# The last chunk's product chain in one PSUM bank or in two, with the order of work rewritten

## The chip, the cores and the metric

The kernel runs on one core of a Trainium2 chip. The core has a matrix engine (TensorE, PE in the profile; PEld is its weight load), VectorE (DVE), ScalarE (ACT), GpSimd (POOL) and SyncE (SP), which only issues transfers. Each engine executes its own instructions strictly in the order given, and waits on semaphores for the others. TensorE writes its results to PSUM, eight banks of 512 fp32 values in each of 128 partitions; VectorE and ScalarE read them there. The other engines' data lie in SBUF. DMA queues move data between HBM and SBUF.

The metric is the device time of one execution in microseconds (us), the median of a few runs.

## The reference

Attention without a softmax over pairs, then a feed-forward block, on 8 batches, 8 heads, 576 tokens, 64 values per head:

```python
q_s = softmax(q, axis=-1)          # over the 64 values of a head
k_s = softmax(k, axis=2)           # over the 576 tokens
kv  = einsum('bhsd,bhse->bhde', k_s, v)
x   = einsum('bhsd,bhde->bhse', q_s, kv)   # to 4608 tokens x 512
h   = x @ w_in                     # 512 x 2048
out = (h * sigmoid(h)) @ w_out     # 2048 x 512, 4608 x 512 fp32
```

## The kernel before, in words

**Tiling.** The 4608 tokens are cut into nine chunks of 512, numbered 0 to 8. Batches have 576 tokens, so a chunk takes its tokens from one or two batches (`pieces`, L266). Chunk 0 is done in a wide form with the 576 tokens of batch 0. From chunk 1 on, the first matrix product, and for chunks 1 to 8 the second, are done by a seven-product scheme on halves (Strassen's in Winograd's form): two halves of the tokens, two of the inner dimension, two of the output, with seven products in place of eight and sums before and after.

**The order table.** The program has a list of named steps, `ORDER` (L18), and issues them one by one (L796). A step's engine is fixed by its function, or by a last letter of the name (`a` ScalarE, `v` VectorE; for stores `s` SyncE, `a` ScalarE, `g` GpSimd). So the table sets each engine's order; between engines only the data and the buffers do. The names that the prediction uses, with `t` a chunk, `b` a batch:

| step | engine | what it does | line |
|---|---|---|---|
| `lq`, `lk`, `lv` b.c | SP (POOL for b < 3) | load half of q, k, v of a batch; two buffers each | L150 |
| `eq`, `ek` b.c | ACT | exp of q, of k | L161, L166 |
| `z` b.c, `n` b.c | DVE, then POOL | sums of exp(q) and their reciprocals; the normalizing product on `eq` | L205, L209, L214 |
| `tq` b | SP | DMA transpose of `eq` to `qT` | L224 |
| `vc` b.c | POOL | cast of v to bf16 | L144 |
| `kv` b, `kc` b | PE, then DVE | k^T v of a batch; division by the sums of exp(k) | L246, L257 |
| `X` t.i | PE | x of the chunk, from `qT` and kv, to banks 0, 1, 6, 7 | L280 |
| `x` t.c, `xs` t.i | ACT or DVE; DVE | x to SBUF; the sums of its halves | L142, L144; L381 |
| `g` t.g.i | PE | product i of the first matrix product, group g; 8 matmuls | L423 |
| `s` t.g.i, `a` t.g.i, `u` t.g.i | ACT or DVE; DVE; ACT | snapshot of the running sum in banks 0 and 1; addition of another product; silu to `GT` | L142, L144; L401; L407 |
| `S` t.i | DVE | the sums of halves of `GT` | L475 |
| `b` t.i.m | PE | product i of the second matrix product for token quarter m of a half; 8 matmuls | L501 |
| `sa`, `sb`, `sc` t | ACT | snapshots of the running sum in bank 4 | L517 |
| `wa`, `wb`, `wc`, `wl` t, `o` t.m | DVE (`wl` either); SP | output sums; their stores | L521, L534, L536; L439 |
| `w`, `h`, `v`, `p`, `m`, `mu`, `tr1`, `T`, `WS`, `po`, `os` | | chunk 0's wide form, chunk 1's first part, batch 1's transposes on TensorE, sums of weights | L305 to L485 |

There is one buffer of `eq` (`exp_q`, L158), so `eq` b waits until batch b-1's transpose has landed. There are three output tiles `ow`; two of `qT`. `exp` and `silu` need different function tables of ScalarE, so each change from the one to the other puts an `ACT_TABLE_LOAD` in front; copies need none.

**PSUM.** The whole of PSUM is one tile, `PS`. Accesses of two engines to the same bank are put one after the other in the order of the program, even where they touch different columns.

**The last chunk.** Chunk 8 (`last`) has its own second product, steps `e` i.m, with i the product and m the half of a 256-token block (128 tokens). Products 1, 6, 7, 4 accumulate one after the other into bank 1 (halves in its two halves), and after 1, 6 and 7 the snapshots `sa8`, `sb8`, `sc8` are taken of the bank (L754). Product 5 goes to banks 4 and 0, 2 to bank 5, 3 to bank 6. Outputs are made in parts of 128 x 256: `waE` (1 + 2), `wxE` and `wbE` (1 + 6 + 5, then + 3), `wcE` (1 + 6 + 7 + 5) on VectorE (L760), and `wlE` (1 + 6 + 7 + 4), a scaled copy of bank 1 by ScalarE or VectorE (L773, L775). Each part is stored in two pieces of 64 rows by `qa`, `qb`, `qc`, `ql` (L778), on the queue that the name's last letter gives.

Of the kernel before, what the change touches and what calls it, by code (L numbers as in the profile page):

```python
# [15 lines left out]


ORDER = """  # L18
    lk1.0 w2 lk1.1 w0 h2 w1 h0 v2 w3 v0 h1 v1 W2b1 w4 h3 v3 w6 h4 WS0.1 w5 h6 WS1.1 W2b2 v4 w7 h5 v5 w8 h7
    v6 w9 lv1.0 h8 v7 WS0.2 w10 h9 v8 eq1.0.0 w11 v9 h10 eq1.0.1 w12 v10 h11 qp1a w13 eq1.1.0 v11 h12 WS0.4  # L20
    qp1b w14 h13 v12 lv1.1 w15 v13 W2c1 WS0.3 p0 W2c2 h15 z1.0 eq1.1.1 p1 v15 n1.0 h14 p2 v14 p3 z1.1.0
    gcopy lq2.0 z1.1.1 tr1.0 ek1.1 lq2.1 p4 n1.1 W2d ek1.0 p5 tc1.0b tc1.0a p6 T1 lk2.0 vc1.0 lk2.1 tr1.1
    WS1.3 p7 lv2.0 vc1.1a vc1.1b tc1.1a tc1.1b kv1 WS1.2 lv2.1 p8 kc1 xt1.0 xt1.1 x1.0a x1.1v p9 x1.2a x1.3v
    g1.1.1 xs1.3 eq2.0 xs1.1 xs1.2 g1.1.2 xs1.4 s1.1.0a z2.0 p10 eq2.1 g1.1.6 a1.1.0 n2.0 p11 s1.1.1a z2.1
    p12 g1.1.7 ek2.0 n2.1 g1.1.5 s1.1.2v p13 a1.1.2 ek2.1 g1.1.4 tq2 WS1.4 p14 vc2.0 p15 u1.1.4 g1.1.3 vc2.1
    po2v po0a lv3.0 m0 po1v u1.1.2 lk3.0 a1.1.1 m1 po3a lk3.1 mu0 lq3.0 m2 T2 mu1 lq3.1 u1.1.1 m3 os0 T4 m4
    mu2 u1.1.0 m5 T3 mu4 os1 kv2 mu5 mu3 m6 vc3.0 kc2 X2.0 mu6 X2.1 lv3.1 x2.1v m7 x2.0a x2.3a x2.2v g2.1.1
    mu7 xs2.1 xs2.2 b1.1.0 xs2.4 xs2.3 s2.1.0v g2.1.2 ek3.0 b1.2.0 S1.1 eq3.0 lk4.0 g2.1.6 lv4.0 S1.2 lq4.0
    b1.1.1 s2.1.1a a2.1.0 b1.2.1 eq3.1 g2.1.7 S1.3 sa1 vc3.1 g2.0.2 s2.1.2a g2.1.5 z3.1 ek3.1 lv4.1 b1.6.0
    lk4.1 a2.1.2 g2.1.4 n3.1 b1.6.1 z3.0 u2.1.4 g2.1.3 sb1 u2.1.0 g2.0.1 n3.0 a2.1.1 b1.7.0 s2.0.0a wa1 kv3  # L30
    u2.1.1 a2.0.0 tq3 g2.0.6 vc4.0 u2.1.2 b1.7.1 s2.0.1v vc4.1 b1.5.0 S1.4 g2.0.7 ek4.0 g2.0.5 sc1 s2.0.2v
    lk5.0 ek4.1 b1.5.1 kc3 eq4.0 g2.0.4 a2.0.2 b1.4.0 lq5.0 wc1 lq4.1 g2.0.3 z4.0 os3 u2.0.4 b1.4.1 lv5.0
    u2.0.0 a2.0.1 b1.3.0 n4.0 os2 wl1a X3.0 X3.1 lk5.1 kv4 x3.0a x3.1v x3.3a x3.2v b1.3.1 u2.0.2 kc4 g3.1.1
# [5 lines left out]
    n5.1 X4.0 X4.1 kv5 x4.0a x4.1v x4.3a wl2v b2.3.1 u3.0.0 x4.2v tq5 g4.1.1 xs4.3 u3.0.1 xs4.1 b3.1.0 wb2  # L39
    s4.1.0a xs4.2 g4.1.2 xs4.4 S3.1 b3.2.0 a4.1.0 ek6.0 g4.1.6 b3.1.1 S3.2 s4.1.1a lk7.0 o2.0 b3.2.1 sa3  # L40
    ek6.1 g4.1.7 g4.1.5 eq6.0 lv6.0 s4.1.2v b3.6.0 eq6.1 lq7.0 a4.1.2 lk7.1 b3.6.1 wa3 g4.1.4 lv6.1 kc5
    g4.1.3 S3.3 u4.1.4 g4.0.2 lq7.1 sb3 a4.1.1 u4.1.0 g4.0.1 z6.0 b3.5.0 s4.0.0a b3.7.0 u4.1.1 a4.0.0 n6.0
    g4.0.6 S3.4 b3.7.1 s4.0.1a g4.0.5 sc3 z6.1 u4.1.2 g4.0.7 vc6.1 b3.4.0 s4.0.2a n6.1 b3.5.1 u4.0.0 a4.0.2
# [10 lines left out]
    g6.0.4 a6.0.2 b5.4.1 u6.0.4 b5.3.0 X7.0 X7.1 x7.0a x7.1v g6.0.3 x7.3a x7.2v u6.0.2 g7.1.1 xs7.1 a6.0.1
    b5.3.1 s7.1.0a xs7.2 g7.1.2 u6.0.1 wl5v g7.1.6 o5.1 a7.1.0 g7.0.2 s7.1.1a xs7.4 xs7.3 b6.1.0 S6.1 o4.1
    b6.1.1 wb5 g7.1.7 sa6 b6.2.0 s7.1.2a g7.1.5 u7.1.0 g7.1.4 a7.1.2 o5.0 b6.2.1 u7.1.4 S6.2 g7.1.3 u7.1.2
    g7.0.1 a7.1.1 b6.6.0 s7.0.0a S6.3 b6.6.1 u7.1.1 wa6 g7.0.6 sb6 a7.0.0 b6.5.0 s7.0.1a b6.7.0 u7.0.0
    g7.0.7 b6.7.1 s7.0.2v g7.0.5 sc6 b6.5.1 a7.0.2 g7.0.4 S6.4 b6.4.0 u7.0.4 b6.4.1 u7.0.2 X8.0 wl6v X8.1
    x8.0a g7.0.3 wc6 x8.3a x8.2v b7.1.0 x8.1v b6.3.0 xs8.3 a7.0.1 b6.3.1 xs8.1 g8.1.1 u7.0.1 xs8.2 wb6
    g8.1.2 s8.1.0a xs8.4 o6.0 S7.1 b7.1.1 g8.1.6 a8.1.0 o6.1 b7.2.0 s8.1.1a S7.2 b7.2.1 sa7 S7.3 g8.1.7 S7.4  # L60
    g8.1.5 s8.1.2a b7.6.0 u8.1.0 a8.1.2 g8.1.4 b7.6.1 u8.1.4 g8.1.3 sb7 g8.0.1 a8.1.1 b7.7.0 s8.0.0a wa7
    b7.7.1 u8.1.1 b7.5.0 u8.1.2 g8.0.6 sc7 g8.0.2 s8.0.1a b7.5.1 a8.0.0 g8.0.7 u8.0.0 g8.0.5 s8.0.2v b7.4.0
# [8 lines left out]
def kernel(  # L71
# [683 lines left out]
    def tile_out(th, n, a):
        return w_out_tile(last, th)[:, a, n * HN:(n + 1) * HN]
# [9 lines left out]
            op1=ALU.add,  # L766
        )

    def part_copy(a, h, w, eng):
        o = tile_out(1, 0, a)[:, h * w:(h + 1) * w]  # L770
        i = PS[:, 1, a * HN + h * w:a * HN + (h + 1) * w]
        if eng is nc.scalar:
            nc.scalar.activation(out=o, in_=i, func=ACT.Copy, scale=OS)  # L773
# [54 lines left out]
```

## Time and profile before

| | |
|---|---|
| median of 3 runs | 259.99 us (259.85 to 260.35) |
| the profiled execution's own time | 259.86 us |
| its span, first to last instruction | 258.1 us |
| granted TensorE clock, mean | 0.995 |
| busy: PE, DVE, ACT, POOL | 249.7, 205.3, 188.5, 64.5 us |
| ACT_TABLE_LOAD | 14, of 1.28 us |

Busy time is the time in which an engine executes; its idle time is set down to what ended it, the releaser. A row of the order of time has the start, the duration, the engine, the line, the operation, output and inputs with their shapes, the count where several are merged, and in brackets the idle time before it with the releaser. An engine with a q, such as SPq, is its sequencer issuing a transfer. TensorE's matmuls overlap, so the end of a merged row can lie after the start of the next.

### The profile page before, as it was taken

To read this page: it belongs to the slowest core of one execution; us is meant where nothing else is said; L and a number is where in the kernel's file an instruction comes from. 1 tells how busy PE (TensorE), PEld (TensorE's weight loads), DVE (VectorE), ACT (ScalarE), POOL (GpSimd) and SP (SyncE) were. 2 spreads that over 40 slices of the span, in tenths; PEclk is the share of its full clock that TensorE was granted. 3 is DMA by queue.
4 is the path that set the end of the run, shared out by engine and by line. 5 is a ranking of instruction groups with operands and counts; after the bars stand their busy time and mean duration, and the time that the engine had idled before them with its cause. 6 is when DMAs were issued, how large, how long until landed. Compare 5 with 4: busy or idle time off the path is not lost.

```text
span 258.1 us, 6452 instructions
## 1 busy us (share of the span) xinstructions
PE 249.7 (97%) x2732; PEld 204.9 (79%) x2732; DVE 205.3 (80%) x278; ACT 188.5 (73%) x222; POOL 64.5 (25%) x62
## 2 busy tenths in 40 slices
...
GB/s 246 343 188 298 298 306 327 302 255 354 387 236 240 343 263 173 144 265 183 259 251 60 225 240 3 3 173 3 0 3 186 60 0 4 163 3 0 73 143 112
DMA packets 35996, 45.89 MB, mean 178 GB/s; under 512 B 16240, under 2 KB 21040, under 8 KB 35968
## 3 DMA queue, kind: packets, MB, share of 16 engines
...
q10 hardware_dynamic: 160, 0.13, 0.2%
...
## 4 chain that ended last, share of the span: by engine, by line
PE 83%; DVE 7%; DMA 4%; ACT 2%; issue 1%; SPq 1%; ACTq 0%; DVEq 0%
PE PS L501 33%; PE PS L423 31%; PE PS L305 6%; PE PS L443 5%; DMA vt<-in_v_dram 4%; PE PS L333 2%; PE PS L246 2%; PE PS L280 2%; DVE h L401 2%; DVE S L475 1%; DVE zq L205 1%; DVE h L144 1%; SPq L150 1%; DMA out_dram<-ow 1%; DVE ow L521 1%
## 5 line engine op out<-in xcount | busy, mean ns | idle before, releaser
L401 DVE TENSOR_TENSOR h<-PS,h 128x1024 f32<-128x1024 f32 (+1 forms) x45 | 54.1, 1205 | 16.8 <-PE PS L423 13.7
L501 PEld LDWEIGHTS <-GT 128*128 128x128 f16 x512 | 50.0, 98 | 5.8
L407 ACT ACTIVATE GT<-h 128x1024 f16<-128x1024 f32 (+1 forms) x45 | 46.7, 1050 | 8.9 <-DVE h L401 8.8
L423 PEld LDWEIGHTS <-WS 128*128 128x128 f16 x480 | 46.7, 98 | 6.7 <-issue 0.9
L501 PE MATMUL PS<-W,GT 128*128 128x256 f16 x384 | 48.0, 273 | 0.0
L423 PE MATMUL PS<-XS,WS 128*128 128x256 f16 (+1 forms) x360 | 44.5, 272 | 0.0
L142 ACT COPY h<-PS 128x1024 f32<-128x1024 f32 (+1 forms) x33 | 33.2, 1005 | 13.5 <-PE PS L423 11.8
L501 PEld LDWEIGHTS <-S 128*128 128x128 f16 x384 | 37.3, 98 | 4.4
L214 POOL TENSOR_TENSOR eq<-eq,rzq 128x1152 bf16<-128x1152 bf16 x13 | 27.5, 2119 | 52.7 <-DVE rzq L209 37.0
L423 PEld LDWEIGHTS <-W 128*128 128x128 f16 x360 | 35.2, 98 | 6.0 <-issue 1.4
L501 PE MATMUL PS<-T,S 128*128 128x256 f16 x256 | 32.2, 273 | 0.0
L423 PE MATMUL PS<-XT,W 128*128 128x256 f16 (+1 forms) x240 | 30.2, 272 | 0.0
L778 POOL DMA_DIRECT2D out_dram<-ow x5 | 2.7, 547 | 89.2 <-DVE ow L760 88.7
L205 DVE TENSOR_REDUCE zq<-eq 128x18 f32<-128x1152 bf16 x14 | 18.8, 1345 | 5.1 <-ACT eq L161 5.1
L407 ACT ACTIVATE GT<-PS 128x1024 f16<-128x1024 f32 (+1 forms) x15 | 15.2, 1015 | 9.2 <-PE PS L423 8.7
L144 POOL CAST vaug<-vt 128x1152 bf16<-128x1152 f32 x12 | 14.2, 1202 | 29.8 <-DMA vt<-in_v_dram 24.6
L161 ACT ACTIVATE eq<-qt 128x1152 bf16<-128x1152 f32 (+1 forms) x18 | 18.9, 1056 | 2.6 <-DMA qt<-in_q_dram 2.5
L166 ACT ACTIVATE ek<-kt 128x1152 bf16<-128x1152 f32 x16 | 18.5, 1161 | 2.3 <-DMA kt<-in_k_dram 2.3
L144 DVE COPY h<-PS 128x1024 f32<-128x1024 f32 (+1 forms) x12 | 14.5, 1208 | 5.9 <-PE PS L423 2.6
L423 PE MATMUL PS<-XS,W 128*128 128x256 f16 (+1 forms) x120 | 15.4, 272 | 1.3 <-ACT h L142 1.3
L501 PE MATMUL PS<-W,S 128*128 128x256 f16 x128 | 16.1, 273 | 0.0
L501 PE MATMUL PS<-T,GT 128*128 128x256 f16 x128 | 16.1, 273 | 0.0
...
## 6 DMA issues: line engine op xcount, KB each, us to landing
...
```

Of the source, the lines that this page charges most:

```text
L142: eng.copy(out=o, in_=i)
L144: eng.tensor_copy(o, i)
L161: nc.scalar.activation(out=half(st[b]["eq"], cc)[:, :, g0:g1], in_=jgd(b, "qt", cc)[:, :, g0:g1], func=ACT.Exp)
L166: nc.scalar.activation(out=half(ek, cc), in_=jgd(b, "kt", cc), func=ACT.Exp)
L205: nc.vector.reduce_sum(out=z, in_=e, axis=AX.X)
L214: eng.tensor_tensor(out=e, in0=e, in1=r[:, :, :, None].to_broadcast([128, J, 2, D]), op=ALU.mult)
L305: nc.tensor.matmul(out=PS[:, WIDE[fb] + n, 0:S // 2], lhsT=W1[:, c, fb * 128:(fb + 1) * 128], rhs=XTS[0][:, c, n * (S // 2):(n + 1) * (S / ...
L401: nc.vector.tensor_tensor(out=four(t, i), in0=group_bank(t, g), in1=four(t, i), op=ALU.add)
L407: nc.scalar.activation(out=group_out(t, f, n), in_=x, func=ACT.Silu, scale=1.0 / XS)
L423: nc.tensor.matmul(out=PS[:, bank + p // 2, (p % 2) * HT:(p % 2) * HT + width(t)], lhsT=a[:, c, p * 128:(p + 1) * 128], rhs=bb[:, c, 0:wid ...
L443: nc.tensor.matmul(out=PS[:, 2 + tb, :], lhsT=GTS[t % 2][:, fc, tb * 128:(tb + 1) * 128], rhs=W2[:, fc, :], start=(fc == 0), stop=(fc == N ...
L501: nc.tensor.matmul(out=PS[:, bank, m * HN:(m + 1) * HN], lhsT=a[:, fc, m * 128:(m + 1) * 128], rhs=bb[:, fc, :], start=(first and fc == 0) ...
```

## The change

Three things change in the last chunk's second product. The chain of products 1, 6, 7, 4 goes to bank 0 for half 0 and to bank 1 for half 1; each snapshot is one instruction that reads half of either bank (`snap_end`); product 5's second half goes to bank 7, product 3's second half to bank 2. `wlE` is one copy of 128 x 256 per half, from its own bank.

The order table is new throughout. Products are the same. Batch 4's transpose (`tq4`) stands ahead of `lq5.1`, `lv5.1`, `lk6.0` and `o1.0`, which it followed, and `z4.1` ahead of `a3.1.0`; `ek5.1` stands before `u3.1.0`; `eq7.0` has moved to late in chunk 5, apart from the other exp steps, so that there are 16 changes of ScalarE's table; the last product is `e3.1` in place of `e4.1`. The core of the diff:

```diff
@@ ORDER @@
...
-    u2.1.1 a2.0.0 tq3 g2.0.6 vc4.0 u2.1.2 b1.7.1 s2.0.1v vc4.1 b1.5.0 S1.4 g2.0.7 ek4.0 g2.0.5 sc1 s2.0.2v
-    lk5.0 ek4.1 b1.5.1 kc3 eq4.0 g2.0.4 a2.0.2 b1.4.0 lq5.0 wc1 lq4.1 g2.0.3 z4.0 os3 u2.0.4 b1.4.1 lv5.0
+    lk4.1 g2.1.4 z3.0 g2.1.3 u2.1.0 g2.0.2 u2.1.4 wa1 n3.0 b1.6.1 a2.1.1 u2.1.2 g2.0.1 sb1 S1.3 kv3 tq3
+    s2.0.0a b1.5.0 kc3 u2.1.1 S1.4 g2.0.6 b1.7.0 s2.0.1v lv4.0 ek4.1 b1.7.1 lv4.1 a2.0.0 os3 g2.0.7 sc1
+    ek4.0 b1.5.1 s2.0.2v g2.0.5 eq4.0 lk5.0 wc1 lq4.1 g2.0.4 a2.0.2 os2 b1.4.0 vc4.0 lk5.1 z4.0 u2.0.4
...
-    xs3.1 u2.0.1 xs3.2 wb1 b2.1.0 s3.1.0a xs3.4 o1.0 g3.1.2 xs3.3 S2.1 b2.1.1 a3.1.0 eq4.1 g3.1.6 lv5.1
-    b2.2.0 S2.2 s3.1.1a lq5.1 g3.1.5 sa2 z4.1 ek5.0 g3.1.7 g3.0.2 s3.1.2v n4.1 b2.6.0 u3.1.0 a3.1.2 g3.1.4
-    tq4 S2.3 b2.6.1 u3.1.4 g3.1.3 sb2 u3.1.2 g3.0.1 a3.1.1 o1.1 b2.2.1 s3.0.0a b2.7.0 wa2 u3.1.1 a3.0.0
-    g3.0.6 b2.7.1 s3.0.1v eq5.0 b2.5.0 S2.4 g3.0.7 ek5.1 lq6.0 lk6.0 z5.0 g3.0.5 s3.0.2a lk6.1 b2.5.1 sc2
-    a3.0.2 n5.0 eq5.1 g3.0.4 wc2 b2.4.0 lq6.1 z5.1 g3.0.3 vc5.0 u3.0.4 b2.4.1 a3.0.1 vc5.1 u3.0.2 b2.3.0
+    b1.3.1 kc4 x3.3a xs3.1 u2.0.1 g3.1.1 xs3.2 wb1 g3.1.2 s3.1.0a xs3.3 xs3.4 g3.0.2 S2.1 g3.1.6 S2.2 eq4.1
+    b2.2.0 s3.1.1a b2.1.0 z4.1 ek5.0 b2.1.1 a3.1.0 g3.1.7 n4.1 sa2 ek5.1 b2.6.0 s3.1.2v g3.1.5 vc5.0 tq4
+    g3.1.4 a3.1.2 u3.1.0 b2.6.1 u3.1.4 S2.3 g3.1.3 sb2 lq5.1 g3.0.1 u3.1.2 a3.1.1 lv5.1 lk6.0 b2.7.0 s3.0.0a
+    o1.0 S2.4 b2.2.1 u3.1.1 a3.0.0 g3.0.6 lv6.0 b2.7.1 s3.0.1v eq5.0 g3.0.5 wa2 g3.0.7 sc2 lq6.0 z5.0 b2.4.0
+    s3.0.2a lk6.1 b2.5.0 vc5.1 eq5.1 a3.0.2 g3.0.4 o1.1 n5.0 z5.1 g3.0.3 u3.0.4 b2.5.1 a3.0.1 n5.1 u3.0.0
...
-    g4.0.4 wc3 g4.0.3 vc6.0 u4.0.4 b3.4.1 a4.0.1 u4.0.2 b3.3.0 wl3v u4.0.1 X5.0 X5.1 kv6 x5.0v x5.1a tq6
-    x5.2v b3.3.1 x5.3v g5.1.1 xs5.1 ek7.1 S4.1 b4.1.0 s5.1.0a lv7.0 xs5.3 g5.1.2 o2.1 xs5.2 ek7.0 wb3 b4.1.1
-    kc6 g5.1.6 a5.1.0 lv7.1 b4.2.0 s5.1.1a S4.2 g5.0.2 sa4 xs5.4 eq7.0 g5.1.7 S4.3 g5.1.5 o3.1 s5.1.2a
-    b4.2.1 eq7.1 a5.1.2 g5.1.4 o3.0 z7.0 b4.6.0 vc7.1 u5.1.4 b4.6.1 wa4 vc7.0 u5.1.0 g5.1.3 n7.0 g5.0.1
-    a5.1.1 b4.5.0 s5.0.0a b4.5.1 sb4 a5.0.0 u5.1.1 g5.0.6 b4.7.0 s5.0.1v b4.7.1 S4.4 g5.0.7 sc4 u5.1.2 z7.1
-    g5.0.5 s5.0.2a b4.4.0 n7.1 b4.4.1 a5.0.2 g5.0.4 wl4a wc4 u5.0.2 g5.0.3 u5.0.4 b4.3.0 a5.0.1 u5.0.0
-    b4.3.1 u5.0.1 X6.0 X6.1 kv7 x6.0v x6.1a x6.3v b5.1.0 x6.2a xs6.1 g6.1.1 wb4 xs6.2 o4.0 b5.1.1 xs6.3
+    u4.0.2 g4.0.3 wc3 n6.0 b3.3.0 u4.0.4 a4.0.1 b3.4.0 u4.0.0 X5.0 X5.1 kv6 x5.0a x5.1v tq6 x5.3a x5.2v
+    b3.3.1 u4.0.1 xs5.1 g5.1.1 xs5.2 wb3 b3.4.1 s5.1.0v o2.1 ek7.1 g5.1.2 kc6 g5.1.6 wl3a xs5.3 xs5.4 a5.1.0
+    lv7.0 b4.2.0 s5.1.1a lv7.1 b4.1.0 S4.1 eq7.1 g5.1.7 ek7.0 b4.2.1 s5.1.2v o3.1 g5.1.5 S4.2 b4.1.1 u5.1.0
+    a5.1.2 g5.1.4 sa4 g5.0.2 o3.0 u5.1.4 wa4 g5.1.3 S4.3 u5.1.2 vc7.1 g5.0.1 b4.6.0 a5.1.1 vc7.0 s5.0.0a
+    b4.6.1 a5.0.0 u5.1.1 g5.0.6 S4.4 b4.5.0 s5.0.1a b4.5.1 sb4 u5.0.0 g5.0.7 g5.0.5 s5.0.2v b4.7.0 eq7.0
+    a5.0.2 b4.7.1 z7.1 g5.0.4 sc4 g5.0.3 b4.4.0 a5.0.1 u5.0.4 b4.4.1 wc4 u5.0.1 X6.0 X6.1 kv7 x6.0v u5.0.2
...
-    a8.0.2 g8.0.4 S8.1a b7.4.1 u8.0.2 wc7 g8.0.3 u8.0.4 b7.3.0 a8.0.1 b7.3.1 wl7v u8.0.1 e1.0 wb7 o7.1 S8.1b
-    e1.1 S8.2a e2.0 S8.2b sa8 o7.0 S8.3 e2.1 e6.0 waE0 S8.4 e6.1 waE1 e5.0 sb8 qa11s e3.0 qa10s wxE0 qa01s
-    e7.0 wbE0 qb01s e7.1 qa00s e5.1 sc8 wcE0 e3.1 wcE1 qc00g wxE1 qc10s e4.0 qc01g wbE1 qb00s qb10g e4.1
-    wlE0a qc11s qb11g ql00a ql01g wlE1xa wlE1yv ql10s ql11a
+    b7.4.1 o7.0 sa8 S8.2b e2.0 S8.3 e6.0 wl7v e6.1 e2.1 sb8 e5.0 waE1 waE0 e7.0 S8.4 qa01s qa11s e7.1 wxE0
+    qa00s e3.0 sc8 o7.1 e5.1 wbE0 wcE0 qb00a e4.0 qc00s e4.1 wlE0v qc01s wcE1 ql00g e3.1 wxE1 qc11s wlE1a
+    ql01g qc10a ql11s qa10g qb01a wbE1 ql10g qb10s qb11a
@@ -739,18 +739,29 @@
     for i in ORDER1:
         for m in range(2):
             if i == 5:
-                op(f"e{i}.{m}", prod, last, i, m, (4, 0)[m], True, True)
+                op(f"e{i}.{m}", prod, last, i, m, (4, 7)[m], True, True)
             elif i == 3:
-                op(f"e{i}.{m}", prod, last, i, m, 6, m == 0, m == 1)
+                op(f"e{i}.{m}", prod, last, i, m, (6, 2)[m], True, True)
+            elif i == 2:
+                op(f"e{i}.{m}", prod, last, i, m, 5)
             else:
-                op(f"e{i}.{m}", prod, last, i, m, 5 if i == 2 else 1)
+                op(f"e{i}.{m}", prod, last, i, m, m, i == 1, i == 4)
     for i in (1, 2):
         op(f"S{last}.{i}a", s_op, last, i, 4, 8)
         op(f"S{last}.{i}b", s_op, last, i, 0, 4)
     for i in (3, 4):
         op(f"S{last}.{i}", s_op, last, i)
+    def snap_end(name):
+        WG[last][name] = mp.tile([128, 512], FP32, name=name, bufs=1)
+        nc.scalar.activation(
+            out=WG[last][name].rearrange("p (a n) -> p a n", a=2),
+            in_=PS.rearrange("p b (a n) -> p (b a) n", a=2)[:, 0:4:3, :],
+            func=ACT.Copy,
+            scale=OS,
+        )
+
     for x in ("sa", "sb", "sc"):
-        op(f"{x}{last}", snap, last, x, 1)
+        op(f"{x}{last}", snap_end, x)
 
     def tile_out(th, n, a):
         return w_out_tile(last, th)[:, a, n * HN:(n + 1) * HN]
@@ -766,9 +777,9 @@
             op1=ALU.add,
         )
 
-    def part_copy(a, h, w, eng):
-        o = tile_out(1, 0, a)[:, h * w:(h + 1) * w]
-        i = PS[:, 1, a * HN + h * w:a * HN + (h + 1) * w]
+    def part_copy(a, eng):
+        o = tile_out(1, 0, a)
+        i = PS[:, a, a * HN:(a + 1) * HN]
         if eng is nc.scalar:
             nc.scalar.activation(out=o, in_=i, func=ACT.Copy, scale=OS)
         else:
@@ -782,16 +793,14 @@
 
     for a in range(2):
         op(f"waE{a}", part, 0, 0, a, 5, "sa")
-        op(f"wcE{a}", part, 1, 1, a, (4, 0)[a], "sc")
-        op(f"wxE{a}", part, 0, 1, a, (4, 0)[a], "sb")
-        op(f"wbE{a}", part, 0, 1, a, 6)
+        op(f"wcE{a}", part, 1, 1, a, (4, 7)[a], "sc")
+        op(f"wxE{a}", part, 0, 1, a, (4, 7)[a], "sb")
+        op(f"wbE{a}", part, 0, 1, a, (6, 2)[a])
+        both(f"wlE{a}", part_copy, a)
         for x, th, n in (("a", 0, 0), ("c", 1, 1), ("b", 0, 1), ("l", 1, 0)):
             for i in range(2):
                 for e, dma in (("s", nc.sync), ("a", nc.scalar), ("g", nc.gpsimd)):
                     op(f"q{x}{a}{i}{e}", part_store, th, n, a, i, dma)
-    both("wlE0", part_copy, 0, 0, HN)
-    both("wlE1x", part_copy, 1, 0, HN // 2)
-    both("wlE1y", part_copy, 1, 1, HN // 2)
 
     for name in ORDER.split():
         ops[name]()
```

More of the change, by code (lines that the diff above doesn't have):

```diff
@@ L18 @@
 ORDER = """
[L19 to L28, printed above, removed]
@@ L29 @@
-    b1.1.1 s2.1.1a a2.1.0 b1.2.1 eq3.1 g2.1.7 S1.3 sa1 vc3.1 g2.0.2 s2.1.2a g2.1.5 z3.1 ek3.1 lv4.1 b1.6.0
-    lk4.1 a2.1.2 g2.1.4 n3.1 b1.6.1 z3.0 u2.1.4 g2.1.3 sb1 u2.1.0 g2.0.1 n3.0 a2.1.1 b1.7.0 s2.0.0a wa1 kv3
-    u2.1.1 a2.0.0 tq3 g2.0.6 vc4.0 u2.1.2 b1.7.1 s2.0.1v vc4.1 b1.5.0 S1.4 g2.0.7 ek4.0 g2.0.5 sc1 s2.0.2v
-    lk5.0 ek4.1 b1.5.1 kc3 eq4.0 g2.0.4 a2.0.2 b1.4.0 lq5.0 wc1 lq4.1 g2.0.3 z4.0 os3 u2.0.4 b1.4.1 lv5.0
-    u2.0.0 a2.0.1 b1.3.0 n4.0 os2 wl1a X3.0 X3.1 lk5.1 kv4 x3.0a x3.1v x3.3a x3.2v b1.3.1 u2.0.2 kc4 g3.1.1
@@ L39 @@
[L39 to L43, printed above, removed]
@@ L54 @@
[L54 to L58, printed above, removed]
@@ L59 @@
[L59 to L62, printed above, removed]
-    a8.0.2 g8.0.4 S8.1a b7.4.1 u8.0.2 wc7 g8.0.3 u8.0.4 b7.3.0 a8.0.1 b7.3.1 wl7v u8.0.1 e1.0 wb7 o7.1 S8.1b
@@ L64 @@
-    e1.1 S8.2a e2.0 S8.2b sa8 o7.0 S8.3 e2.1 e6.0 waE0 S8.4 e6.1 waE1 e5.0 sb8 qa11s e3.0 qa10s wxE0 qa01s
-    e7.0 wbE0 qb01s e7.1 qa00s e5.1 sc8 wcE0 e3.1 wcE1 qc00g wxE1 qc10s e4.0 qc01g wbE1 qb00s qb10g e4.1
-    wlE0a qc11s qb11g ql00a ql01g wlE1xa wlE1yv ql10s ql11a
+    lk1.0 w1 lk1.1 w2 h1 w0 h2 v1 w3 h0 W2b1 w5 v0 v2 h3 w4 WS0.1 h5 w6 v3 h4 W2b2 v4 w7 v5 w8 h7 h6 v7 w9
+    lv1.0 h8 v6 w11 v8 h9 lv1.1 w10 eq1.0.0 v9 h11 WS0.2 w12 eq1.1.0 v11 h10 w13 WS1.1 eq1.0.1 v10 h12 w15
+    qp1a h13 v12 w14 eq1.1.1 v13 qp1b WS1.2 W2c1 p0 h14 z1.0 ek1.0 p1 z1.1.0 n1.0 z1.1.1 p2 h15 ek1.1 v15 p3
```

31 lines of the change are left out of this document (28 added, 3 removed).

## The prediction

> **What bounds the kernel now.** I read the page's header and busy shares first, then stretches cut at the X steps, then who waits for whom, then the order of time around each hole.
>
> ```profile
> span 258.1 us, 6452 instructions
> ...
> PE 249.7 (97%) x2732; PEld 204.9 (79%) x2732; DVE 205.3 (80%) x278; ACT 188.5 (73%) x222; POOL 64.5 (25%) x62
> ```
>
> TensorE is idle for 258.1 - 249.7 = 8.4 us. The stretches say where:
>
> ```profile
> 84.85:112.06 27.21, 25.95 (x316) 22.97 (x320) 23.91 (x31) 24.91 (x28) 8.20 (x6) 1.00 0.81 241
> 112.06:138.20 26.14, 26.04 (x316) 23.00 (x320) 23.11 (x29) 23.73 (x27) 8.25 (x5) 1.00 0.64 200
> 138.20:164.80 26.60, 26.60 (x324) 23.71 (x327) 21.80 (x29) 21.82 (x25) 6.46 (x4) 1.00 0.52 127
> ...
> 253.10:258.10 5.00, 0.00 (x0) 0.00 (x0) 0.29 (x1) 0.65 (x2) 0.68 (x2) 0.76 0.41 111
> ```
>
> Columns are the stretch, its length, then busy time of PE, PEld, DVE, ACT and POOL, clock, DMA. Chunk 3 (X3 to X4) has a hole of 27.21 - 25.95 = 1.26; chunk 4 one of 0.10; the tail after the last product is 5.0; the other 2.0 lie before 20 us. In chunk 3 ScalarE is busy 24.91 of 27.21: it has little to spare.
>
> ```profile
> 100.28 1.06 ACT L407 ACTIVATE GT<-h 128x1024 f16<-128x1024 f32 x1
> 103.07 1.28 ACT L161 ACT_TABLE_LOAD   x1 [1.73 <-DMA qT<-eq]
> 104.36 1.16 ACT L161 ACTIVATE eq<-qt 128x1152 bf16<-128x1152 f32 x1
> 105.43 1.15 ACT L166 ACTIVATE ek<-kt 128x1152 bf16<-128x1152 f32 x1
> 106.49 0.99 ACT L142 COPY h<-PS 128x1024 f32<-128x1024 f32 x1
> ```
>
> ```profile
> 105.23 1.04 PE L501 MATMUL PS<-T,S 128*128 128x256 f16 x8
> 107.53 1.03 PE L423 MATMUL PS<-XS,W 128*128 128x256 f16 x8 [1.26 <-ACT h L142]
> ```
>
> In order of time: ScalarE, done with u3.1.1 at 101.34, waits 1.73 for batch 4's transpose (eq is one buffer), loads its table, does eq5.0 and ek5.1, and only then the snapshot s3.0.2a that g3.0.4 on TensorE waits for. The transpose itself, on SyncE:
>
> ```profile
> 96.62 2.54 SPq L224 DMA_TRANSPOSE qT<-eq  x1
> ```
>
> ```profile
> DMA to landing us min/median/max: 4.6/4.7/6.4
> ```
>
> Batch 4's is the 6.4: issued at 96.62, landed at 103.0. The tail:
>
> ```profile
> 251.15 1.91 PE L501 MATMUL PS<-T,GT 128*128 128x256 f16 x16
> ```
>
> ```profile
> 253.09 0.38 ACT L773 ACTIVATE ow<-PS 128x256 f32<-128x256 f32 x1 [2.84 <-DMA out_dram<-ow]
> 253.51 0.55 ACTq L778 DMA_DIRECT2D out_dram<-ow  x1
> 254.10 0.28 ACT L773 ACTIVATE ow<-PS 128x128 f32<-128x128 f32 x1 [0.62 <-ACT ow L773]
> 254.73 0.50 ACTq L778 DMA_DIRECT2D out_dram<-ow  x1
> ```
>
> The first copy starts 0.03 after e4.1's end (251.15 + 1.91 = 253.06), though its own half, e4.0, was ready 0.87 sooner; I read the named DMA as a coincidence. Three copies and a store's issue follow one another, and the last stores are issued 1.67 after the last product; the span ends 3.35 after that.
>
> **Part by part.** Products, matmuls and their 0.873 us per group of 8 are the same in both tables, 282 steps each on TensorE; the clock is 1.00 throughout. What can move is the holes.
>
> *Batch 4's transpose.* I walk chunk 3 in the new order, from X3.0 at 84.85 as before: X pair 0.56, kv4 0.64, 27 groups of 0.873 and 0.11 for the first, so X4.0 is due at 109.7. ScalarE's steps from start to start: silu 0.93, exp 1.07, snapshot h 0.90, sa/sb/sc 0.49, and 1.41 more where the function changes between exp and silu (eq4.0 80.45 to u2.0.4 82.91 is 1.07 + 1.39). s3.1.0a waits for g3.1.1 and starts at 87.95; eq4.1 90.25, s3.1.1a 91.3, ek5.0 92.2, sa2 93.3 to 93.9 (b2.6.0 is due at 94.0), ek5.1 93.8, u3.1.0 96.3, u3.1.4 97.2 to 98.2 (g3.0.1 due 98.4), s3.0.0a 99.5 (g3.0.6 due 101.0), u3.1.1 100.4, eq5.0 102.8, sc2 103.9 to 104.5 (b2.4.0 due 104.5), s3.0.2a 104.4 to 105.4 (g3.0.4 due 106.2), u3.0.4 to 108.8 (X4.0 due 109.7). On VectorE z4.1 now precedes a3.1.0: eq4.1's end 91.4, z4.1 1.64, n4.1 on GpSimd 2.12, so the transpose is issued at 95.35, 1.3 sooner, and lands at 100.0 with 4.7, at 101.7 with 6.4. eq5.0's table load wants it by 101.4. ek5.1, 1.07, is moved out from between eq5.0 and s3.0.2a. Both together cover the 1.26, and I take all of it: -1.26; ends 0 and -1.36 (with chunk 4's 0.10).
>
> What the transpose is moved past: o1.0's four issues (0.6 each) and lq5.1, lv5.1 now stand behind its 2.5 on SyncE's queue, at 98 instead of 89 to 93. Loads land about 5 later, 103 and 104; eq5.1 is due at 105.3, kv5's cast of v needs it by 109, and o1.0's buffer is wanted by wc2 after 107. lv4.0 and lv4.1, moved behind tq3, go out at about 76 and land by 82; both casts end by 83.4, kv4 is due at 85.4. All hidden, by margins of 2 us and more. GpSimd's n5.0 now waits behind vc5.1, which ends at 105.6, when z5.0 ends too. Nothing.
>
> *The two banks.* Both snapshots stay one instruction of 128x512, 0.60. New tail, with E the end of the last product, e3.1: e4.1 ends at E-0.87, e4.0 at E-1.75. VectorE: wlE0 E-1.7, wcE1 E-1.3, wxE1 E-0.9, all 0.42, then wbE1 E+0.03 to E+0.45. ScalarE's wlE1 is over at E-0.45. So arithmetic ends 0.45 after the last product instead of 1.64. But SyncE's queue then ends last: qa01s waits for waE0 (e2.1 ends E-7.0, waE1 and waE0 after it) and starts at E-6.05; one issue of 0.51 and two of 0.64, o7.1's four of 0.64, then qc00, qc01, qc11, ql11 and qb10 of 0.64, so qb10 is issued at E+0.86 instead of 254.73 - 253.06 = 1.67. ScalarE's qb11 goes out at E+0.7, GpSimd's last at E+0.5 (0.6 each). Thirteen stores of 64 KB and o7.1 share the last 6 us, which may lengthen the landing: the loneliest took 1.94 from issue, those next to GpSimd's 2.3 to 2.6. Ends +0.2 (landing 0.9 longer) and -0.8; I take -0.5, nearest to the issue times, less 0.3 for the crowding that the rows show.
>
> *The rest of the table.* Walked with the same durations, VectorE reaches kc1 at 40.3 against 40.16 before, and xt1.0 is due 0.1 after its first part; h15 behind ek1.0 lets v15 end at 34.5, when tr1.0 is due. In chunk 2 g2.1.6 (due 63.05) has 0.15 after s2.1.0v, g2.1.7 0.1 after s2.1.1a, g2.1.3 0.2, and others 0.4. Chunks 4, 6, 7 and 8 show 0.3 or more at each wait that I followed; the tail 0.5 (S8.4 before e3.0). So no hole is due, but some eight places have 0.1 or 0.2, and a record starts 0.03 to 0.1 after its releaser. I take +0.3; ends 0 (before, the same kind of margin cost 0.10 in three chunks) and +1.3 (the one hole of before, come back elsewhere).
>
> *Chunk 5's switches.* The exp steps there are in two groups instead of one: 4 table loads instead of 2, 16 instead of 14 in all. By the trace's step this is 2 x 1.41 = 2.8 us more of ScalarE, in a chunk where it was busy 21.82 of 26.60. The tight place: u5.0.0 154.15, eq7.0 156.5, sc4 when b4.7.1 ends, 158.05, table, u5.0.4 159.95 to 160.97; X6.0, which overwrites its bank, is due at 161.5 (X5.0 at 135.7). Cost nothing; if the cover of 0.5 goes, what is missing.
>
> The Trainium skill, ScalarE: Activation LUTs, What ACT_TABLE_LOAD costs, has a load of 1283 ns and a drain of some 1380 ns, 2.66 in all; the load agrees with the 1.28 above, the drain shows nowhere in the 1.41. By its 2.66, u5.0.4 would end at 163.0 and X6.0 wait 1.5, and the sum below would be 260.0.
>
> **The sum.** The profiled execution took 259.86 (span 258.08 and 1.78 around it), 0.13 under the median 259.99. -1.26 - 0.5 + 0.3 = -1.46: 258.4 on its own time, 258.5 against the median.
>
> **Rivals.** (a) The gain is given back in tenths: the eight narrow places lose 1.3 to 2 us together, as ScalarE must stay on time through chunks 2 and 3 (54.6 us of it to 51 of TensorE's, by the page's means). For it: that load. Against it: TensorE's 26.60 without a hole in chunk 5. 259.8 to 260.5.
>
> (b) The wait moves to batch 3's transpose, and the kernel is slower. eq4.0 is now reached at 79.4 (80.45 before), and tq3, issued at 73.5 by the walk, lands at 78.2 with 4.7, at 79.9 with 6.4. If its sums on VectorE or GpSimd's n3.0 are late and it lands at 82, ScalarE is 2.6 late into u2.0.4 and chunk 3, where the margin is 0.1 to 0.4: TensorE stands 2.4. -1.46 + 2.4: 260.9. It decides from a landing at about 81.5. Before, eq4.0 had 1.07 after its landing at 79.38: against it.
>
> (c) The switches of chunk 5 cost more than 1.41. If one cost its load twice (2.56, 1.15 more), eq7.0 would end at 158.7, sc4 start 0.67 later, u5.0.4 end at 160.97 + 0.67 + 1.15 = 162.8, and X6.0 wait 1.3: 259.8. The 14 switches of before, at 1.41, are against it. The rule of the Trainium skill's page ScalarE: Activation LUTs, named above, is of this kind.
>
> (d) The transpose is not sooner: eq4.1 or z4.1 comes late by the 1.3, and eq5.0 waits as before. The tail remains: 259.5 to 259.8.
>
> **How the numbers follow.** Forecast 0.55, (a) 0.18, (b) 0.17, (c) 0.05, (d) 0.05. A measurement of this kernel tells about 0.2%, 0.5 us, from no change. Faster: 0.55, a third of (a), half of (d): 0.63. Same: 0.12. Slower: 0.25, (b) and parts of (a) and (c). The forecast's own range is 257.8 (1.36 and 0.8, no new waits) to 259.2; with (a), (c), (d) and the nearer part of (b) 257.8 to 260.6.
>
> **What would show it.** Right: batch 4's transpose issued before 96, no DMA wait ahead of eq5.0's table load, chunk 3 with TensorE busy but for 0.3, PE's busy end near 251.9 to 252.2, and last arithmetic 0.5 after it, with SyncE's queue issuing on for another 0.4. Wrong: a PE wait over 0.5 on ScalarE's h, sa or sc, or on GT L407 before X6.0; a wait of eq on qT at 80; a last landing over 3.5 after the last product.

## The result, and the profile after

Over 20 runs of each, the changed kernel takes 259.23 us (median; 258.52 to 260.35), the kernel before 259.86 (259.53 to 260.91). The ratio is 0.9975, with an interval of 0.9963 to 0.9986: about 0.65 us faster, where 1.46 was forecast. The profiled execution took 258.91 us, with a span of 256.86.

The header and the busy shares of the changed kernel:

```profile
span 256.9 us, 6450 instructions
...
PE 248.4 (97%) x2732; PEld 204.5 (80%) x2732; DVE 205.3 (80%) x276; ACT 191.4 (75%) x225; POOL 64.9 (25%) x61
```

Its stretches, cut at its own X3.0, X4.0, X5.0 and X6.0, and the end from the last product on (stretch, length, then busy time and count of PE, PEld, DVE, ACT and POOL, clock, DMA share, GB/s):

```profile
84.52:109.65 25.13, 25.13 (x306) 22.17 (x306) 23.51 (x30) 24.25 (x27) 9.42 (x6) 1.00 0.81 266
109.65:135.41 25.76, 25.76 (x314) 22.99 (x314) 22.29 (x29) 23.05 (x26) 8.07 (x5) 1.00 0.77 227
135.41:161.17 25.76, 25.76 (x314) 22.95 (x313) 22.59 (x27) 23.26 (x26) 3.47 (x3) 1.00 0.50 131
251.20:256.90 5.70, 0.01 (x1) 0.00 (x0) 0.42 (x1) 0.00 (x0) 1.21 (x3) 0.73 0.48 129
```

TensorE is busy for the whole of all three chunks: the hole of 1.26 in chunk 3 is gone, and so is the 0.10 of chunk 4. Products have moved between the stretches, so their lengths can't be compared with those of before one by one. The loss is in the last row. Calling E the end of the last product, the tail from E to the end of the span was 258.08 - 253.06 = 5.02 before; it is now 256.86 - 251.21 = 5.65.

The order of time on ScalarE, around the place of the hole:

```profile
100.23 1.07 ACT L407 ACTIVATE GT<-h 128x1024 f16<-128x1024 f32 x1
101.32 1.28 ACT L161 ACT_TABLE_LOAD   x1
102.62 1.16 ACT L161 ACTIVATE eq<-qt 128x1152 bf16<-128x1152 f32 x1
103.69 0.58 ACT L517 ACTIVATE sc<-PS 128x512 f32<-128x512 f32 x1
104.41 1.01 ACT L142 COPY h<-PS 128x1024 f32<-128x1024 f32 x1
```

The table load for eq5.0 carries no bracket: it follows u3.1.1 at once. No ek5.1 stands between eq5.0 and the snapshot s3.0.2a, which starts at 104.41 instead of 106.49. The transpose, on SyncE:

```profile
95.21 2.76 SPq L224 DMA_TRANSPOSE qT<-eq  x1
```

It is issued 1.41 sooner than before, and had landed at 99.84. Now the tail, again in order of time:

```profile
249.51 3.52 SPq L789 DMA_DIRECT2D out_dram<-ow  x5
...
250.18 1.04 PE L501 MATMUL PS<-W,S 128*128 128x256 f16 x8
...
250.23 2.18 POOL L789 DMA_DIRECT2D out_dram<-ow  x4 [72.12 <-DVE ow L786]
...
250.44 1.86 ACTq L789 DMA_DIRECT2D out_dram<-ow  x3
251.25 0.42 DVE L771 SCALAR_TENSOR_TENSOR ow<-PS,ow 128x256 f32<-128x256 f32 x1 [0.66 <-PE PS L501]
```

The arithmetic is over at 251.67, 0.46 after E, where before it went on to E + 1.64. SyncE's last issue starts at 252.08 (E + 0.87; before, the last was ScalarE's at E + 1.67). From there the end should come sooner; it does not. The last landing is at 255.32, 3.24 after that issue, and the chain that ended last, read from E - 2.3 on, runs elsewhere:

```profile
249.50 0.44 DVE ow L786
...
250.23 0.92 POOL out_dram L789 x2
...
251.36 0.53 POOL out_dram L789
251.88 0.52 POOLq L832
```

It ends on GpSimd's stores and its queue, not on the last product. This view counts GpSimd's issues as work of the engine, those of SyncE and ScalarE not, so it is only a hint. The rows of the program's end decide, line 823 before and line 832 now (x: count; ns, least, median, most; first and last start):

```profile
L823 POOLq EVENT_SEMAPHORE  x4: 17/17/17, 257.3 to 258.0; - x4
L823 POOLq DRAIN  x3: 51/93/3204, 253.7 to 257.8; - x3
L823 SPq DRAIN  x3: 7/7/7, 257.2 to 257.6; - x3
```

```profile
L832 POOLq EVENT_SEMAPHORE  x4: 17/17/17, 256.1 to 256.8; - x4
L832 POOLq DRAIN  x3: 51/102/4440, 251.6 to 256.6; - x3
L832 SPq DRAIN  x3: 7/7/13, 255.5 to 256.3; - x3
```

Each engine's list ends with such drains. One of GpSimd's three takes 4.44 in the changed kernel: it starts at 251.63 and ends at 256.07, 0.75 after the last landing and 1.15 after GpSimd's own last landing (254.92). Behind it GpSimd waits, in the first of its four semaphore instructions, for SyncE, which checks the landings one by one and gives its signal with the second of its drains. In all ten profiles of this document this wait is over 0.03 after SyncE's second drain or 0.04 after GpSimd's long one, whichever ends later, and the span ends 0.73 to 0.75 after that. Before, GpSimd's long drain ended at 256.95 and SyncE's second at 257.32: SyncE, and so the last landing (256.93), decided. Now SyncE is done at 255.59 and GpSimd's drain, 256.07, decides, 0.5 later. The stores of the last 64 KB pieces, by queue, with the median from issue to landing at the end of each row:

```profile
out_dram<-ow SPq DMA_DIRECT2D x8, 64.0 KB, 2.4
out_dram<-ow ACTq DMA_DIRECT2D x4, 64.0 KB, 3.2
out_dram<-ow POOLq DMA_DIRECT2D x4, 64.0 KB, 2.9
```

Before, SyncE's nine took 2.1 and GpSimd's five 2.2.

### The profile page after: what moved, and what is told of

It reads as the page before. It is cut to its first block, busy times and chain, and to the rows that moved or that the text cites. A ratio compares the mean times of both kernels' runs of the same rounds, so it can differ in the third digit from the quotient of the medians.

```text
span 256.9 us, 6450 instructions
## 1 busy us (share of the span) xinstructions
PE 248.4 (97%) x2732; PEld 204.5 (80%) x2732; DVE 205.3 (80%) x276; ACT 191.4 (75%) x225; POOL 64.9 (25%) x61
## 4 chain that ended last, share of the span: by engine, by line
PE 91%; DMA 4%; SPq 1%; ACT 1%; POOL 1%; issue 0%; POOLq 0%; DVE 0%
PE PS L501 38%; PE PS L423 36%; PE PS L305 6%; PE PS L443 5%; DMA vt<-in_v_dram 4%; PE PS L333 2%; PE PS L280 2%; PE PS L246 2%; SPq L150 1%; POOL out_dram L789 1%; PE PS L232 0%; ACT vaug L142 0%; ACT XT L142 0%; ACT qT L142 0%; POOLq L832 0%
## 5 line engine op out<-in xcount | busy, mean ns | idle before, releaser
L142 ACT COPY h<-PS 128x1024 f32<-128x1024 f32 (+1 forms) x32 | 32.1, 1004 | 18.9 <-PE PS L423 17.7
L423 PE MATMUL PS<-XS,WS 128*128 128x256 f16 (+1 forms) x360 | 45.2, 272 | 0.0
L144 POOL CAST vaug<-vt 128x1152 bf16<-128x1152 f32 x12 | 15.7, 1323 | 59.5 <-DMA vt<-in_v_dram 59.1
L144 DVE COPY h<-PS 128x1024 f32<-128x1024 f32 (+1 forms) x13 | 15.8, 1212 | 7.3 <-ACT GT L407 2.9
L305 PE MATMUL PS<-XT,W 128*128 128x288 f16 x128 | 15.9, 286 | 0.0
```

The source lines that it names most:

```text
L142: eng.copy(out=o, in_=i)
L144: eng.tensor_copy(o, i)
L305: nc.tensor.matmul(out=PS[:, WIDE[fb] + n, 0:S // 2], lhsT=W1[:, c, fb * 128:(fb + 1) * 128], rhs=XTS[0][:, c, n * (S // 2):(n + 1) * (S / ...
L423: nc.tensor.matmul(out=PS[:, bank + p // 2, (p % 2) * HT:(p % 2) * HT + width(t)], lhsT=a[:, c, p * 128:(p + 1) * 128], rhs=bb[:, c, 0:wid ...
```

## The experiments

The theory was that the new order removes the stall and the end of the new table gives most of it back. All times below are medians beside the kernel before on the same chip (260.18 in the first four runs, 260.00 in the last four); us are the ratio times 260. Lines in the first seven experiments are 4 higher than in the kernel whose code they share.

**The new table without its tail.** The changed kernel, but from `b7.4.1` on with the tail of before, and the one-bank code of before:

```diff
-    wc7 a8.0.2 b7.4.0 u8.0.4 b7.3.0 S8.2a u8.0.2 g8.0.3 u8.0.0 e1.0 a8.0.1 b7.3.1 u8.0.1 e1.1 wb7 S8.1b
...
+    wc7 a8.0.2 b7.4.0 u8.0.4 b7.4.1 u8.0.2 g8.0.3 u8.0.0 b7.3.0 a8.0.1 b7.3.1 wl7v u8.0.1 e1.0 wb7 o7.1
...
+    qb11g ql00a ql01g wlE1xa wlE1yv ql10s ql11a
```

> The changed kernel's order table up to the last chunk's second product, then the tail of before: one bank for the chain, wlE in three copies, the old stores. In the changed kernel's profile the stretch from the end of the last product to the end of the span is 5.65 us, 5.02 in before. Theory: the new order gains 1.84 us ahead of the tail and the new tail loses 0.63; so this kernel has its last product's end at 251.2, a span of 256.2 and a time 1.8 to 1.9 us under before. Rival: the new tail's two banks do gain, and the 0.63 is an accident of that execution; then this kernel has a span of 257.3 or more and is only 0.7 us under before.

Measured: 258.57, ratio 0.9940 (0.9926 to 0.9954), so 1.56 gained; tail 5.04, TensorE's end at 251.55. Without the new tail the table gains more than twice what the whole change does, and the two intervals do not meet: by time the new tail costs about 0.9, or 0.7 against the changed kernel's second measurement (the last run below).

**One step moved in the old table.** The kernel before, with ek5.1 alone moved:

```diff
-    g3.0.6 b2.7.1 s3.0.1v eq5.0 b2.5.0 S2.4 g3.0.7 ek5.1 lq6.0 lk6.0 z5.0 g3.0.5 s3.0.2a lk6.1 b2.5.1 sc2
+    g3.0.6 b2.7.1 s3.0.1v ek5.1 eq5.0 b2.5.0 S2.4 g3.0.7 lq6.0 lk6.0 z5.0 g3.0.5 s3.0.2a lk6.1 b2.5.1 sc2
```

> The kernel before with one step moved: ek5.1 stands ahead of eq5.0, so that ScalarE does it (table load included) while it waits for batch 4's transpose. Theory: the hole of 1.26 us in chunk 3 is the whole of what that wait costs; eq5.0 starts at 103.7 instead of 104.36, s3.0.2a at 104.8 instead of 106.5, g3.0.4 (due at 106.27) finds it done: TensorE has no hole there, the last product ends at 251.8, and the time is 1.2 to 1.3 us under before. Rival: the hole is one execution's, and most executions have a smaller one, since a transpose takes 4.6 to 6.4 us; then the time is only some 0.6 us under before, as the changed kernel's is.

Measured: 258.64, ratio 0.9943 (0.9929 to 0.9956): 1.48. ScalarE in order of time, and a stretch that ends behind chunk 3 (this kernel's X3.0 starts at 84.59, its X4.0 at 110.47):

```profile
100.19 1.06 ACT L411 ACTIVATE GT<-h 128x1024 f16<-128x1024 f32 x1
101.27 1.28 ACT L170 ACT_TABLE_LOAD   x1
102.56 1.16 ACT L170 ACTIVATE ek<-kt 128x1152 bf16<-128x1152 f32 x1
103.63 1.15 ACT L165 ACTIVATE eq<-qt 128x1152 bf16<-128x1152 f32 x1
104.69 0.99 ACT L146 COPY h<-PS 128x1024 f32<-128x1024 f32 x1
```

```profile
84.75:110.90 26.15, 26.15 (x328) 23.28 (x321) 23.73 (x31) 25.18 (x27) 7.71 (x5) 1.00 0.83 246
```

ek5.1 reads nothing of the transpose, so with ek5.1 first the table load and 1.07 of work lie in the time of the wait, and the hole is gone with the transpose where it was. This single swap is worth as much as the whole new table without its tail (1.48 and 1.56, well inside each other's interval). The rest of the rewriting neither gains nor loses anything that can be told.

**GpSimd's late stores given to the others.** The changed kernel, with o7.1 sooner, GpSimd's four small stores early, and the late ones on SyncE and ScalarE:

```diff
-    b7.4.1 o7.0 sa8 S8.2b e2.0 S8.3 e6.0 wl7v e6.1 e2.1 sb8 e5.0 waE1 waE0 e7.0 S8.4 qa01s qa11s e7.1 wxE0
-    qa00s e3.0 sc8 o7.1 e5.1 wbE0 wcE0 qb00a e4.0 qc00s e4.1 wlE0v qc01s wcE1 ql00g e3.1 wxE1 qc11s wlE1a
-    ql01g qc10a ql11s qa10g qb01a wbE1 ql10g qb10s qb11a
+    b7.4.1 o7.0 sa8 S8.2b e2.0 S8.3 e6.0 wl7v o7.1 e6.1 e2.1 sb8 e5.0 waE1 waE0 e7.0 S8.4 qa10g qa11g qa00g
+    qa01g e7.1 wxE0 e3.0 sc8 e5.1 wbE0 wcE0 qb00a qb01a e4.0 qc00s qc01s e4.1 wlE0v ql00s ql01s wcE1 e3.1
+    wxE1 wlE1a qc11s qc10a ql11s ql10a wbE1 qb11s qb10a
```

> The changed kernel with another share-out of the same stores: o7.1 right after wl7v (some 4 us sooner on SyncE), GpSimd issues the four earliest stores (qa) and none of the last ones, SyncE and ScalarE the other twelve. Theory D: the end waits for GpSimd, whose closing drain ends 1.15 us after its last store has landed; without late stores of its own the end is the last landing plus 1.15: the last issue is at 252.3, landing 2.6 later or less: 254.9, end 256.0, a tail of 4.8 instead of 5.65, time 0.8 under the changed kernel. Rival C: the stores slow each other, whoever issues them: the last lands 3.2 after its issue, and the tail stays at 5.4 to 5.7.

Measured: 258.16, ratio 0.9927 (0.9909 to 0.9945): 1.9. The tail is 4.46, although the last issue starts later than in the changed kernel (E + 1.41 against 0.87): it landed 2.01 later. The stores by queue, and the end of the chain:

```profile
out_dram<-ow SPq DMA_DIRECT2D x7, 64.0 KB, 2.0
out_dram<-ow ACTq DMA_DIRECT2D x5, 64.0 KB, 2.0
out_dram<-ow POOLq DMA_DIRECT2D x4, 64.0 KB, 2.1
```

```profile
247.98 3.29 PE PS L505 x30
251.27 0.02 issue
251.29 0.42 DVE ow L775
```

The chain ends with the product and the arithmetic again, and the stores of every queue land in 2.0 to 2.1 (medians). The edit does three things at once: o7.1 goes sooner, GpSimd stores early, and the late stores are shared out anew. The next run has the first alone.

**o7.1 alone sooner.** The same tail as the changed kernel's, with only `o7.1` moved from after `sc8` to after `wl7v`.

> The changed kernel with o7.1's four issues of 128 KB right after wl7v, ahead of qa on SyncE, and nothing else: half a megabyte leaves the last 5 us, GpSimd's four late stores stay. Theory D: GpSimd's last store is issued at 251.9 and its drain ends 1.15 us after its landing, so the tail stays at 5.2 to 5.6. Rival C: without the crowd each store lands 2.0 to 2.3 after its issue, SyncE's last is issued at 251.9, and the tail falls to 4.3 to 4.5.

Measured: 259.05, ratio 0.9966 (0.9949 to 0.9982): 0.88. In the profile the last landing comes at E + 3.43 instead of E + 4.11, and the tail is 5.19 instead of 5.65. Its stores:

```profile
out_dram<-ow SPq DMA_DIRECT2D x8, 64.0 KB, 2.1
out_dram<-ow ACTq DMA_DIRECT2D x4, 64.0 KB, 2.6
out_dram<-ow POOLq DMA_DIRECT2D x4, 64.0 KB, 2.6
```

So 5.65 becomes 5.19 by o7.1's place, and 5.19 becomes 4.46 when GpSimd's stores leave the end as well and the others share the late ones. By time the first of these is not told from nothing (0.88 against the changed kernel's 0.65 to 0.86). This execution was also late at its start, a wait of 0.40 for weights at 19.6 us, which the edit does not touch.

**The two banks alone.** The old table with the code of the changed kernel:

```diff
-    wlE0a qc11s qb11g ql00a ql01g wlE1xa wlE1yv ql10s ql11a
+    wlE0a qc11s qb11g ql00a ql01g wlE1v ql10s ql11a
```

> The order table of before, unchanged but for wlE1, which is one copy on VectorE instead of two; the last chunk's chain in two banks. Theory: with the stores as before, two banks alone shorten the tail, since wlE0 then needs only e4.0 and starts 0.84 us before the last product's end, and wlE1 ends 0.45 after it instead of 1.64; the last stores are issued 1.2 sooner, GpSimd's last one (ql01) too, so the tail is 3.8 instead of 5.02 and the time 1.2 us under before; the hole of 1.26 in chunk 3 stays. Rival: the last stores meet qc and qb on the queues and land later by as much as they are issued sooner, as in the changed kernel; the tail is 4.6 to 5.0 and the time within 0.4 us of before.

Measured: 259.33, ratio 0.9976 (0.9965 to 0.9986): 0.62. The tail is 4.46 instead of 5.02. In order of time:

```profile
251.09 1.91 PE L505 MATMUL PS<-T,GT 128*128 128x256 f16 x16
...
252.16 0.38 ACT L788 ACTIVATE ow<-PS 128x256 f32<-128x256 f32 x1 [1.96 <-PE PS L505]
252.58 1.41 ACTq L793 DMA_DIRECT2D out_dram<-ow  x2
253.04 0.42 DVE L790 TENSOR_SCALAR ow<-PS 128x256 f32<-128x256 f32 x1 [1.19 <-PE PS L505]
```

wlE0 now starts when its own product e4.0 is done, at E - 0.84, and not at E + 0.03 as the one-bank code made it; one copy is left after E. This is the gain the prediction gave to the banks, in the old table, which still has its hole in chunk 3 (1.24, up to 107.5). It is half of the 1.2 expected for this kernel: the last issue is 1.2 sooner, but now GpSimd's drain, at E + 3.68, decides the end.

**Both.** The old table with `ek5.1` moved and the two banks.

> The same with ek5.1 ahead of eq5.0, the step that took the hole in chunk 3 away. Theory: the two gains add up, 1.5 (measured for the step) and 1.2 (the tail): 2.7 us under before. Rival: with the tail at 4.6 to 5.0, 1.5 to 1.9 under before.

Measured: 258.02, ratio 0.9919 (0.9902 to 0.9936): 2.1, the sum of 1.48 and 0.62, and not the 2.7 expected; tail 4.47. With two places of the old table altered it does better than the whole new table does.

**Both, and no late store on GpSimd.** The former, with the end of the table anew; `qa11g qa10g qa01g qa00g` are GpSimd's four:

```diff
-    sa8 o7.0 S8.3 e2.1 e6.0 waE0 S8.4 e6.1 waE1 e5.0 sb8 qa11s e3.0 qa10s wxE0 qa01s e7.0 wbE0 qb01s
...
-    wlE0a qc11s qb11g ql00a ql01g wlE1v ql10s ql11a
+    sa8 o7.0 S8.3 e2.1 e6.0 waE0 S8.4 e6.1 waE1 e5.0 sb8 qa11g e3.0 qa10g wxE0 qa01g e7.0 wbE0 qb01s
+    e7.1 qa00g qb00s e5.1 sc8 wcE0 e3.1 wcE1 qc00s wxE1 qc10a e4.0 qc01s qc11a wbE1 qb10s qb11a
+    e4.1 wlE0v ql00s ql01a wlE1v ql10s ql11a
```

> The same again, with GpSimd issuing the four earliest stores (qa) and none of the late ones, both wlE on VectorE, and the late stores shared by SyncE and ScalarE so that no queue is behind when the last part is ready. Theory D (GpSimd's closing drain ends 1.15 us after its last store's landing): the last issue is 0.47 after the last product, lands 2.0 to 2.3 later, and the end follows 1.03 after that: a tail of 3.5 to 3.8, and 2.7 to 2.9 us under before. If GpSimd's drain is not on the path in the kernel with two banks and the old share-out, the two are alike; if it is, this one is 0.3 to 0.7 faster than that.

Measured: 257.56, ratio 0.9900 (0.9883 to 0.9916): 2.6 faster than before, and the best of all. The tail is 3.79, against 4.47 in the former; by time the step is worth 0.46, and the two intervals still overlap. The edit also moves wlE0 from ScalarE to VectorE; the arithmetic ends at E + 0.46 in both. The end of the chain:

```profile
248.91 3.07 PE PS L505 x28
251.98 0.03 issue
252.00 0.42 DVE ow L790
```

GpSimd's long drain ended at 250.56, before the last product; the last landing is at 254.67, 2.06 after its issue.

**The changed kernel once more**, unaltered, on the same chip as the last three.

> The changed kernel itself, profiled once more beside the others. Theory: its tail is set by the crowd of stores and GpSimd's drain, not by one execution's accident: last issue 0.87 after the last product, last landing 4.0 to 4.2 after it, GpSimd's drain 0.5 to 0.8 later still, tail 5.5 to 5.8. Rival: the tail is 5.0 or less this time, and the 0.63 is not the kernel's.

Measured: 259.27, ratio 0.9967 (0.9955 to 0.9980): 0.86. In its profile the tail is 5.62 and the last landing again at E + 4.11, with the last issue at E + 0.88, so the long tail is no accident of one execution. This execution took 260.71. It lost its time at the start; from 37 us on TensorE has no hole. What TensorE waited for:

```profile
PE PS L246 <- ACT vaug L142: 1.4, 2, 1.2
...
PE PS L305 <- DMA W<-in_moe_w_in_dram: 0.5, 1, 0.5
```

The tails together (us; landing and drain counted from E; the drain is GpSimd's long one, where it ends after E):

| kernel | tail | last issue | last landing | drain's end | us gained |
|---|---|---|---|---|---|
| before | 5.02 | 1.67 | 3.87 | 3.89 | - |
| changed | 5.65 | 0.87 | 4.11 | 4.86 | 0.65 |
| changed, once more | 5.62 | 0.88 | 4.11 | 4.83 | 0.86 |
| new table, old tail | 5.04 | 1.69 | 3.89 | 3.90 | 1.56 |
| ek5.1 moved alone | 5.06 | 1.68 | 3.89 | 3.89 | 1.48 |
| o7.1 sooner | 5.19 | 0.67 | 3.43 | 4.42 | 0.88 |
| GpSimd early | 4.46 | 1.41 | 3.42 | - | 1.9 |
| two banks alone | 4.46 | 0.49 | 2.90 | 3.68 | 0.62 |
| banks, ek5.1 | 4.47 | 0.50 | 2.83 | 3.69 | 2.1 |
| same, GpSimd early | 3.79 | 0.64 | 2.70 | - | 2.6 |

In the three kernels with the old tail the last landing, a store of ScalarE, and GpSimd's drain come together; SyncE decides, and the tail is 1.15 to 1.17 more than the last landing. In the other five in which GpSimd stores late its drain outlasts SyncE's checks, and the tail is the drain's end and 0.77 to 0.79 more. Where GpSimd stores early, the tail is the last landing and 1.04 to 1.09 more.

## Why the prediction was right or wrong

The sign was right. The time, 259.23, lies within the wide range with the rivals (257.8 to 260.6), and 0.03 beyond the forecast's own (257.8 to 259.2). Of the gain, less than half came: two terms were about right or too cautious, and one, the new tail's, came out with the other sign.

**Batch 4's transpose: right.** It was issued at 95.21 (forecast 95.35) and landed at 99.84 (100.0), eq5.0 started at 102.62 (102.8), s3.0.2a at 104.41 (104.4), X4.0 at 109.65 (109.7). The stall was worth about 1.5 in time, both in the new table without its tail and with the one swap; 1.26 lies within both intervals. The text gave the gain to the sooner transpose and to ek5.1's place together. The runs show that ek5.1's place alone is enough; whether the sooner transpose alone is enough was not run. What the transpose was moved past cost nothing: no hole is left behind it.

**The two banks: the step that failed.** The term was -0.5; in the changed kernel's two profiles the tail is 0.60 and 0.63 longer, and by time the new tail costs about 0.9 against the old. The banks themselves were sized rightly: alone they take 0.56 off the tail and 0.62 off the time. The arithmetic of the new tail and its last issue were right too, at E + 0.46 and E + 0.87 against E + 0.45 and E + 0.86. What the step missed is what stands behind the last issue. It let the last store land as before, in 1.94, plus 0.3 for the crowding; it landed 3.24 after its issue, 1.0 more than that. And it left the rest of the end a constant. In the kernel before that rest went by SyncE, and GpSimd's drain, though it ended as late as the last landing, had 0.35 to spare; the prediction did not look at it. In the new tail the drain decides by 0.5. An estimate from these rows: with SyncE's signal deciding (255.59) the tail would have been 5.15, so the late landing alone ate the banks' gain and the drain came on top. In the new tail all four of GpSimd's small stores wait for wlE0 and stand at the very end, qa10g among them, whose data (waE1, over by 245.1) were ready 6 us before its issue; the drain then ended 0.75 after everything had landed. The warning sign named, a last landing over 3.5 after the last product, is what came, at 4.10; it was a weak sign, as the kernel before already had 3.87.

**The rest of the table: +0.3 was not due.** TensorE has no hole above 0.1 between 15 us and the last product, so the eight narrow places cost nothing. TensorE's end, 251.21, lies 0.9 ahead of the 252.1 that the terms add up to (253.06 - 1.26 + 0.3), and 0.7 ahead of the nearer bound named: the 0.3 above, 0.26 by which X3.0 was already sooner (its first matmul at 84.52, before at 84.78), and chunk 4's 0.10; some 0.2 stay open.

**Chunk 5's switches: right, cost nothing.** ScalarE in chunk 5 of the changed kernel:

```profile
155.06 1.28 ACT L161 ACT_TABLE_LOAD   x1
156.35 1.16 ACT L161 ACTIVATE eq<-qt 128x1152 bf16<-128x1152 f32 x1
157.78 0.60 ACT L517 ACTIVATE sc<-PS 128x512 f32<-128x512 f32 x1 [0.27 <-PE PS L501]
158.40 1.28 ACT L407 ACT_TABLE_LOAD   x1
159.69 1.02 ACT L407 ACTIVATE GT<-PS 128x1024 f16<-128x1024 f32 x1
```

eq7.0 came at 156.35 (forecast 156.5), u5.0.4 ended at 160.71 (160.97), and X6.0 stood at 161.17 with no wait. Each switch costs its load of 1.28 and a gap of 0.01 or 0.02 around it. The 2.66 of the Trainium skill, ScalarE: Activation LUTs, What ACT_TABLE_LOAD costs, does not show in this chunk any more than in the kernel before; the measurement decides.

**The rivals.** (b) and (d) did not come: batch 3's transpose landed at 78.46, eq4.0 started at 79.24 without a wait, and batch 4's was sooner. (c) did not come, by the rows above. (a) gave nearly the right kind of loss, part of the gain given back, but by the wrong place: there are no lost tenths in the chunks, the loss is whole and at the end.

The measured terms, -1.5 for the stall, +0.6 to +0.9 for the tail and nothing for the rest, make -0.6 to -0.9, and the two measurements gave -0.65 and -0.86.

**Open.** Between the tails (0.6) and the times (0.9) of the changed kernel and of the new table with the old tail some 0.3 remain (0.1 by the second measurement), within the intervals. The starts of the executions differ by more than that, as the last run shows. Why a store lands later while GpSimd's are under way was not separated: it could be GpSimd's issuing, its larger packets, or three queues storing at once.
